# Idle TensorE products between the first dispatch products, and five tiles' rows kept until most of a table is written

## The chip, the cores and the metric

The kernel runs on one core of a Trainium2 chip. The time is the device time of one execution in microseconds; the median of three runs is the measure. Besides the timed runs there is one execution with a profile.

## The reference

```python
def reference(q, k, v, ...):
    attn = local_attention(q, k, v) + pooled_attention(q, k, v)      # 4 x 8 heads x 576 x 64
    x = attn.transpose(0, 2, 1, 3).reshape(2304, 512)
    x = soft_moe(x, phi, moe_w1, moe_w2)                             # 8 experts x 4 slots
    # second layer of experts: two of eight for each token
    noisy = x @ w_gate + log1p(exp(x @ w_noise)) * noise
    top2, top2_w = two largest of noisy and their softmax
    for e in range(8):
        for k in range(2):
            mask = top2[:, k] == e
            out[mask] += top2_w[mask, k, None] * (relu(x[mask] @ w1[e]) @ w2[e])
    return out                                                       # 2304 x 512
```

Both edits lie in the second layer of experts (w1 is 512 x 1024, w2 1024 x 512 for each expert).

## The kernel before, in words

Attention and the first layer of experts fill the first 212 us. Since every token is then a mixture of 32 slots, the second layer works on the mixing weights: `stk` holds for each of 18 token tiles of 128 tokens a row per token with those weights, the gates and the token's number, 128 numbers in all. For each expert up to 640 tokens (`CAP`) are collected, 128 x 5 tiles. So there are 40 output tiles, `tile2(e, ti)` for expert e and ti from 0 to 4. Each is a row of 24 products of 512 columns on TensorE into a PSUM tile `y` (two buffers), and between them the instructions of the list `fill[ti]` are issued, spread evenly: this is how all other work is ordered by hand. Instructions run in the order of issue on each engine.

How tokens are collected:

- Experts 0 and 1: by products. `onehot(e, n)` lets VectorE compare a token tile's ranks with a ramp, `dispatch(e, n)` multiplies `stk` with the result on TensorE. For expert 0 the one-hots 0 to 9 and their dispatches run ahead of the first output tile (L1178, L1185), the others, 10 to 17, lie in tile 0's list, which is written out as `FILL0` (`f` first layer, `w` split of w2, `o` one-hot, `s` scatter, `g` product for expert 1, `d` dispatch).
- Experts 2 to 7: through a table `tab` in DRAM. `places` works out a row number for each token and choice, then 36 `scatter`s (an indirect DMA of 128 rows issued by GpSimd, each behind a small memset called `spacer`) write `stk` into the table: eight by FILL0, 28 by the list `SCAT`, whose entries (tile, from, to) put scatters into the lists of tiles 1 to 6 (tile number 5e + ti). `xfetch(e)` reads 640 rows into a tile `XT` (two buffers), `turn` transposes them on TensorE, `gathered` copies them to `XS` on ScalarE, `first_layer` multiplies and applies relu. For expert 2, xfetch lies in tile 8's list, turn, gathered and first_layer in tile 9's. The read waits for all scatters, and on SyncE's queue reads of later experts' weights stand behind it.

At the end of `tile2` ScalarE writes the tile times its gates to `ys` (three buffers), and `add_out` adds its rows to the output: an indirect DMA with an add, issued by GpSimd. Output rows of one expert differ, so `add_out` lifts the dependence on the add just before it within the expert:

```python
        if ti:
            tc.declare_no_dep(st.ins, AD[e, ti - 1].ins, reason="an expert has a token once")
```

All other adds to the output keep their order by waiting. The list `OUTS` holds tiles whose add has not been issued yet: in the kernel before, tiles 0 and 1 of expert 0 are kept and added behind tile 2, and every later tile is added at once.

`spin(n)` issues n products of 512 bf16 columns into a `y` buffer that nobody reads. `SPIN[5]` of them stand behind the first dispatches.

Of the kernel before, what the change touches and what calls it, by code (L numbers as in the profile page):

```python
# [7 lines left out]
F32 = mybir.dt.float32  # L8
# [30 lines left out]
def attn_moe_moe_kernel(ctx: ExitStack, tc: tile.TileContext, q, k, v, moe_phi, moe_w1, moe_w2,  # L39
# [4 lines left out]
    DM = H * D  # L44
# [42 lines left out]
    for r in range(0, out.shape[0], 512):  # L87
        n = min(512, out.shape[0] - r)
# [27 lines left out]
    with ExitStack() as tctx:  # L116
# [48 lines left out]
        LD, VQ, KD, DQ, SD, SS, PD, PL, XL, XT, XK = ({} for _ in range(11))  # L165
# [470 lines left out]
        for nm in TSEQ:  # L636
# [4 lines left out]
            else:  # L641
                n, u = nm.split(":")
# [173 lines left out]
    wkp = sctx.enter_context(tc.tile_pool(name="ewk", bufs=2, reuse_waits="tile"))  # L816
# [81 lines left out]
    def dispatch(e, n):  # L898
        i = ORD[n]
        lo, hi = WIN[i]  # L900
        if n == 0:
            XP[e] = [ps.tile([128, n], F32, name=f"xs{c}", bufs=1) for c, (_, n) in enumerate(CH)]
        oh = OH.pop((e, n))
        c1 = CH[1][0]
        if lo < c1:
            nc.tensor.matmul(XP[e][0][:, lo:min(hi, c1)], stk[:, i], oh[:, 0:min(hi, c1) - lo], start=(n == 0),
                             stop=True, skip_group_check=True)
        if hi > c1:
            nc.tensor.matmul(XP[e][1][:, max(lo, c1) - c1:hi - c1], stk[:, i], oh[:, max(lo, c1) - lo:hi - lo],
                             start=(i == FIRST1), stop=True, skip_group_check=True)  # L910

    def gathered(e, part=(1, 0)):
        if e not in XS:
            XS[e] = wkp.tile([128, CAP], F32R, name="XS", bufs=1)
        for c in part:
            c0, n = CH[c]
            nc.scalar.activation(XS[e][:, c0:c0 + n], XP[e][c], AF.Copy)
# [23 lines left out]
    XFS = (3, 4)  # L941
    OHG = ()
    WSA = {0: (6, 8, 10, 12, 14, 16), 1: (2, 5, 8, 11, 14, 17)}
    SCAT = [(1, 8, 14), (2, 14, 19), (3, 19, 24), (4, 24, 28), (5, 28, 32), (6, 32, 36)]

    def places():

# [27 lines left out]
    XT = {}  # L975
# [33 lines left out]
    def tile2(e, ti, fill):  # L1009
        c = 0 if 128 * ti < CH[1][0] else 1  # L1010
        nf = len(fill)
        lead = LEAD0 if e == 0 and ti == 0 else 0
        for i in range(lead):
            fill[i]()
        done = lead
        hh, hl = HH[e, c]
        whi, wlo = WS[e]
        ts_ = slice(128 * ti - CH[c][0], 128 * ti - CH[c][0] + 128)
        y = ps.tile([128, DM], F32, name="y")
        for m in range(24):  # L1020
            kk, li = divmod(m, 3)
            l, r_ = ((hh, whi), (hh, wlo), (hl, whi))[li]
            nc.tensor.matmul(y, l[:, kk, ts_], r_[:, kk], start=(m == 0), stop=(m == 23))  # L1023
            while done < nf and (done - lead) * 24 < (m + 1) * nf:
                fill[done]()
                done += 1
        ys = wkp.tile([128, DM], F32, name="ys", bufs=3)
        gt, idx = ME[e]
        nc.scalar.activation(ys, y, AF.Copy, scale=gt[:, ti:ti + 1])  # L1029
        OUTS.append((e, ti, ys))  # L1030
        if e or ti >= 2:
            while OUTS:
                add_out(*OUTS.pop(0))

    OUTS = []

# [2 lines left out]
    def add_out(e, ti, ys):  # L1039
        gt, idx = ME[e]  # L1040
        nc.gpsimd.memset(spacer, 0.0)  # L1041
        st = nc.gpsimd.indirect_dma_start(out=out, out_offset=bass.IndirectOffsetOnAxis(ap=idx[:, ti:ti + 1], axis=0),  # L1042
                                          in_=ys, in_offset=None, compute_op=ALU.add)
        if ti:
            tc.declare_no_dep(st.ins, AD[e, ti - 1].ins, reason="an expert has a token once")
        AD[e, ti] = st
        if (e, ti) in DRAINS:
            nc.gpsimd.drain()  # L1048

    def spin(n):  # L1050

        t = ps.tile([128, DM], F32, name="y") if n else None
        for _ in range(n):
            nc.tensor.matmul(t, onesb, onesb[:, None].to_broadcast([128, 4, 128]), start=True, stop=True)
# [12 lines left out]
    NOH = LAST0 + 1  # L1067
    LEAD0 = 3

    with ExitStack() as gctx:  # L1070
# [13 lines left out]
        t = ps.tile([128, 2 * E], F32, name="h")  # L1084
# [7 lines left out]
        for q_ in range(5):  # L1092
            n = min(4, NTILE - 4 * q_)
# [64 lines left out]
        for i in range(NTILE - 1):  # L1158
            n = NTILE - 1 - i
# [24 lines left out]
            f()  # L1184
        for n in range(NOH):  # L1185
            dispatch(0, n)
        spin(SPIN[5])
        gathered(0, (0,))
        if PLP is None:
# [24 lines left out]
    for e in range(E):  # L1214
# [3 lines left out]
        def add(i, fn, *a):  # L1218
            fill[i].append(lambda: fn(*a))
# [57 lines left out]
        if e == 3:  # L1277
            add(1, spill)
            add(2, spill_n)
        for sl, n0, n1 in SCAT:  # L1280
            if sl // 5 == e:
# [3 lines left out]
        for ti in range(5):  # L1285
            tile2(e, ti, fill[ti])
# [5 lines left out]
    with tc.If(ov > 0):  # L1292
        with ExitStack() as octx:
# [6 lines left out]
            with tc.For_i(0, E, 1) as ei:  # L1300
# [13 lines left out]
                for i in range(NTILE):  # L1314
# [12 lines left out]
                    ys = ow.tile([128, DM], F32, name="oys")  # L1327
# [36 lines left out]
```

## Time and profile before

| | us |
|---|---|
| median of three runs | 514.25 |
| lowest, highest | 513.48, 517.23 |
| profiled execution | 509.43 |
| its span, first to last instruction | 506.9 |

The mean granted clock of TensorE over the span is 0.948 of full speed. Times in rows are microseconds from the start of the span; PE is TensorE, PEld its weight load, DVE VectorE, ACT ScalarE, POOL GpSimd, SP SyncE, a q behind a name means that engine's sequencer; L1042 is line 1042 of the kernel. A matmul's shown duration includes its way through the array, so that neighbouring ones overlap; the distance between two starts is what one costs. The releaser that a row names is inferred and can be wrong where several things were waited for.

### The profile page before, as it was taken

The numbers are of one execution on the slowest core, as the hardware profiler recorded it, in microseconds if no ns is written. First come the engines' busy times: TensorE is split into PE (matmuls) and PEld (weight loads), VectorE is DVE, ScalarE is ACT, GpSimd is POOL, SyncE is SP. The second block draws the span as 40 slices with busy tenths as digits, with TensorE's granted clock in tenths as the row PEclk, the third lists the DMA queues.
The fourth block names the chain that finished last, engine by engine and source line by source line (L and its number), as shares of the span: only waits on it lengthen the run. The fifth ranks groups of instructions, "written<-read, shape, count | busy, mean of one in ns | idle before, by whom it ended". The sixth has DMA issues, their size and how long they took to land.

```text
span 506.9 us, 12610 instructions
## 1 busy us (share of the span) xinstructions
PE 462.6 (91%) x4869; PEld 350.5 (69%) x4869; DVE 277.8 (55%) x682; ACT 284.5 (56%) x728; POOL 209.6 (41%) x321
## 2 busy tenths in 40 slices
PE   5787889899698899999999989999999999999993
PEld 4676657767566544446888768788787887878882
DVE  7786566888776432089677326265462552634400
ACT  3788566798687311265556356384662755636410
POOL 4666444656545100128878861322122222222222
PEclk9889877999988999887999999999999999999998
DMA  8999999999999799999994369896856867333333
GB/s 190 279 249 273 229 223 243 256 221 236 270 225 321 272 326 396 395 358 288 354 333 76 65 177 348 260 313 138 233 127 166 255 102 195 43 43 41 41 44 44
DMA packets 89672, 109.56 MB, mean 216 GB/s; under 512 B 30666, under 2 KB 59338, under 8 KB 89610
## 3 DMA queue, kind: packets, MB, share of 16 engines
q1 hardware_dynamic: 82698, 95.87, 64.3%
q0 software_dynamic: 6912, 12.85, 16.8%
q8 instruction: 40, 0.66, 0.6%
q14 instruction: 22, 0.18, 0.1%
HBM read 88.64 MB, written 20.05 MB: 214 GB/s over the span
## 4 chain that ended last, share of the span: by engine, by line
PE 58%; DMA 18%; issue 6%; POOL 6%; DVE 5%; ACT 4%; POOLq 1%; SPq 1%; ACTq 0%; DVEq 0%
PE y L1023 34%; DMA ld<-in_q_dram 5%; DMA wr<-in_moe_w_dram 4%; DMA vq<-in_v_dram 4%; PE yacc L776 3%; DMA ld<-in_k_dram 3%; POOL tab L969 3%; PE hp L754 3%; POOL out_dram L1042 2%; PE gx L828 2%; PE t L214 2%; PE h L1003 2%; PE gx L1003 2%; DMA V<-in_v_dram 1%; POOLq L1048 1%
## 5 line engine op out<-in xcount | busy, mean ns | idle before, releaser
L1023 PE MATMUL y<-whi,hl 128*128 128x512 f32 x320 | 127.7, 399 | 0.0
L1023 PE MATMUL y<-wlo,hh 128*128 128x512 f32 x320 | 127.6, 399 | 0.0
L1023 PE MATMUL y<-whi,hh 128*128 128x512 f32 x320 | 126.8, 396 | 0.3 <-ACT hh L1004 0.3
L1042 POOL DMA_INDIRECT out_dram<-ys,idx x40 | 64.4, 1611 | 114.5 <-ACT ys L1029 63.9
L995 DVE TENSOR_TENSOR wlo<-wr,whi 128x512 fp32r<-128x512 f32 x64 | 41.9, 691 | 54.1 <-ACT whi L992 53.8
L1023 PEld LDWEIGHTS y<-wlo,hh 128*128 128x128 f32 x320 | 60.5, 189 | 13.9 <-issue 1.2
L1029 ACT ACTIVATE ys<-y,gt 128x512 f32<-128x512 f32 x40 | 27.4, 685 | 74.6 <-issue 40.2
L1023 PEld LDWEIGHTS y<-whi,hl 128*128 128x128 f32 x320 | 60.5, 189 | 11.9 <-issue 1.6
L1023 PEld LDWEIGHTS y<-whi,hh 128*128 128x128 f32 x320 | 60.5, 189 | 11.7 <-ACT hh L1004 0.6
L1005 DVE SCALAR_TENSOR_TENSOR hl<-h,hh 128x256 fp32r<-128x256 f32 (+1 forms) x64 | 31.4, 490 | 21.4 <-ACT hh L1004 19.8
L969 POOL DMA_INDIRECT tab<-stk,pos x36 | 36.5, 1015 | 8.4 <-issue 7.6
L294 POOL TENSOR_TENSOR P<-El,su 64x350 f32<-64x350 f32 x31 | 24.1, 778 | 37.8 <-DVE su L287 28.8
L1004 ACT ACTIVATE hh<-h 128x256 fp32r<-128x256 f32 (+1 forms) x64 | 27.9, 436 | 16.4 <-PE h L1003 14.4
L992 ACT ACTIVATE whi<-wr 128x512 fp32r<-128x512 f32 x64 | 36.9, 625 | 0.2
L1005 DVE SCALAR_TENSOR_TENSOR hl<-gx,hh 128x256 fp32r<-128x256 f32 (+1 forms) x64 | 31.3, 489 | 10.2 <-ACT hh L1004 8.1
L1004 ACT ACTIVATE hh<-gx 128x256 fp32r<-128x256 f32 (+1 forms) x64 | 28.0, 438 | 15.2 <-PE gx L1003 12.9
L214 PE MATMUL t<-idf,ld 96*128 96x96 f32 x192 | 23.5, 269 | 12.6 <-DMA ld<-in_k_dram 8.1
L1041 POOL MEMSET spacer<- 1x1 f32 x40 | 18.2, 454 | 39.5 <-issue 39.5
L202 ACT ACTIVATE K<-t 64x288 f32<-64x288 f32 x64 | 27.4, 428 | 8.0 <-PE t L214 6.5
L202 ACT ACTIVATE PT<-t 64x256 f32<-64x256 f32 (+1 forms) x50 | 20.6, 416 | 17.8 <-PE t L336 16.9
L214 PEld LDWEIGHTS t<-idf,ld 96*128 96x128 f32 x192 | 19.0, 153 | 16.6 <-DVE mask L141 3.7
L226 DVE TENSOR_REDUCE Dq<-Q 64x144 f32<-64x576 f32 x32 | 23.9, 747 | 10.2 <-ACT Q L202 9.5
(293 smaller groups left out, 828.8 us busy)
## 6 DMA issues: line engine op xcount, KB each, us to landing
wr<-in_moe_w_dram SPq DMA_DIRECT2D x120, 256.0 KB
wr<-in_moe_w_dram SPq DMA_DIRECT2D x56, 512.0 KB
out_dram<-zero SPq DMA_DIRECT2D x5, 1024.0 KB
V<-in_v_dram SPq DMA_DIRECT2D x62, 80.0 KB
ld<-in_k_dram SPq DMA_DIRECT2D x16, 288.0 KB
ld<-in_q_dram SPq DMA_DIRECT2D x16, 288.0 KB
vq<-in_v_dram SPq DMA_DIRECT2D x16, 288.0 KB
tab<-zero SPq DMA_DIRECT2D x1, 1920.0 KB
```

Source lines behind the costliest of these rows:

```text
L202: nc.scalar.activation(dst, src, AF.Copy)
L214: nc.tensor.transpose(t[:, c:288:3], ld[:, i, h, 128 * c:128 * c + 128], idf[0:96, 0:96])
L226: nc.vector.tensor_reduce(out=Dq[hs, :, h], in_=Q[hs, h, 0:576].rearrange("p (a n r) -> p a n r", a=3, r=4), axis=AX.X, op=ALU.add)
L294: eng.tensor_tensor(P[as_, :, HQ * a:HQ * a + KW], El[as_], su[as_, :, None].to_broadcast([64, NG, KW]), op=ALU.mult)
L969: st = nc.gpsimd.indirect_dma_start(out=tab, out_offset=bass.IndirectOffsetOnAxis(ap=pos[:, c, i:i + 1], axis=0), in_=stk[:, i].bitcast(F3 ...
L992: nc.scalar.activation(whi[:, kk], wb(kk), AF.Copy)
L995: eng.tensor_tensor(wlo[:, kk], wb(kk), whi[:, kk].bitcast(F32), op=ALU.subtract)
L1004: nc.scalar.activation(hh[:, f], h, AF.Relu)
L1005: nc.vector.scalar_tensor_tensor(hl[:, f], h, 0.0, hh[:, f].bitcast(F32), op0=ALU.max, op1=ALU.subtract)
L1023: nc.tensor.matmul(y, l[:, kk, ts_], r_[:, kk], start=(m == 0), stop=(m == 23))
L1029: nc.scalar.activation(ys, y, AF.Copy, scale=gt[:, ti:ti + 1])
L1042: st = nc.gpsimd.indirect_dma_start(out=out, out_offset=bass.IndirectOffsetOnAxis(ap=idx[:, ti:ti + 1], axis=0), in_=ys, in_offset=None, c ...
```

## The change

Behind each of the first nine dispatches of expert 0 one idle product is issued, two behind the first. The first five tiles are kept: tiles 0 and 1 in buffers of XT, which stand empty until tile 8, the others in ys. At tile 4 the adds of tiles 0 to 2 are issued, at tile 5 that of tile 3, at tile 6 those of tiles 4 to 6, and from tile 7 on each at once. (`SCAT[-1][0]` is 6.) The list of the scatters starts with five instead of six in tile 1, so that tile 4 has five instead of four.

```diff
--- before.py
+++ after.py
@@ -941,7 +941,7 @@
     XFS = (3, 4)
     OHG = ()
     WSA = {0: (6, 8, 10, 12, 14, 16), 1: (2, 5, 8, 11, 14, 17)}
-    SCAT = [(1, 8, 14), (2, 14, 19), (3, 19, 24), (4, 24, 28), (5, 28, 32), (6, 32, 36)]
+    SCAT = [(1, 8, 13), (2, 13, 18), (3, 18, 23), (4, 23, 28), (5, 28, 32), (6, 32, 36)]
 
     def places():
 
@@ -1024,13 +1024,16 @@
             while done < nf and (done - lead) * 24 < (m + 1) * nf:
                 fill[done]()
                 done += 1
-        ys = wkp.tile([128, DM], F32, name="ys", bufs=3)
+        if e == 0 and ti < 2:
+            ys = wkp.tile([128, 5, 128], F32, name="XT").rearrange("p t d -> p (t d)")[:, 0:DM]
+        else:
+            ys = wkp.tile([128, DM], F32, name="ys", bufs=3)
         gt, idx = ME[e]
         nc.scalar.activation(ys, y, AF.Copy, scale=gt[:, ti:ti + 1])
         OUTS.append((e, ti, ys))
-        if e or ti >= 2:
-            while OUTS:
-                add_out(*OUTS.pop(0))
+
+        while len(OUTS) > (5 if 5 * e + ti < 4 else 2 if 5 * e + ti < SCAT[-1][0] else 0):
+            add_out(*OUTS.pop(0))
 
     OUTS = []
 
@@ -1184,6 +1187,8 @@
             f()
         for n in range(NOH):
             dispatch(0, n)
+            if n + 1 < NOH:
+                spin(1 + (n == 0))
         spin(SPIN[5])
         gathered(0, (0,))
         if PLP is None:
```

## Rows read from the trace of the kernel before

**Rows 1.** The page: busy time, share of the span and instructions of each engine.
```profile
PE 462.6 (91%) x4869; PEld 350.5 (69%) x4869; DVE 277.8 (55%) x682; ACT 284.5 (56%) x728; POOL 209.6 (41%) x321
```

**Rows 2.** Waits of TensorE, 230 us to the end: us, times, longest.
```profile
PE xs L984 <- DMA XT<-tab: 1.6, 1, 1.6
```

**Rows 3.** The chain that ended last, 290 to 300 us: start, us, what.
```profile
294.59 2.25 DMA tab<-stk,pos
296.86 3.17 DMA XT<-tab
```

**Rows 4.** GpSimd's timeline, 259 to 300 us: start us, us, instruction, idle before it.
```profile
259.82 2.10 POOL L1042 DMA_INDIRECT out_dram<-ys,idx  x1 [0.22 <-ACT whi L992]
...
266.15 1.57 POOL L1042 DMA_INDIRECT out_dram<-ys,idx  x1 [2.25 <-ACT whi L992]
...
268.02 0.99 POOL L969 DMA_INDIRECT tab<-stk,pos  x1 [0.26 <-issue]
...
293.32 0.96 POOL L969 DMA_INDIRECT tab<-stk,pos  x1 [0.22 <-issue]
...
294.59 0.95 POOL L969 DMA_INDIRECT tab<-stk,pos  x1 [0.23 <-issue]
...
295.85 1.62 POOL L1042 DMA_INDIRECT out_dram<-ys,idx  x1 [0.23 <-issue]
...
297.77 2.11 POOL L1042 DMA_INDIRECT out_dram<-ys,idx  x1 [0.27 <-ACT whi L992]
```

**Rows 5.** Windows, 229 to 236 us: busy by engine; granted clock, DMA share, GB/s.
```profile
229.40:236.20 6.80, 6.49 (x19) 5.07 (x20) 6.58 (x13) 3.19 (x8) 5.53 (x12) 0.50 1.05 296
```

**Rows 6.** TensorE's timeline, 221 us: idle products.
```profile
220.84 1.47 PE L1054 MATMUL y<-onesb 128*128 128x512 bf16 x6
```

**Rows 7.** TensorE's timeline, 228 us: dispatch products.
```profile
228.11 0.36 PE L906 MATMUL xs<-oh,stk 128*128 128x192 f32 x1 [0.24 <-DVE oh L891]
...
228.75 0.36 PE L906 MATMUL xs<-oh,stk 128*128 128x192 f32 x1 [0.23 <-DVE oh L891]
```

**Rows 8.** Windows, 225 to 242 us: the third busy time is VectorE.
```profile
225.05:233.00 7.95, 6.35 (x30) 4.08 (x20) 7.95 (x15) 5.25 (x14) 6.96 (x13) 0.78 1.03 302
233.00:242.40 9.40, 9.40 (x50) 6.86 (x50) 8.97 (x22) 4.37 (x11) 7.66 (x14) 0.83 1.02 282
```

**Rows 9.** Adds (L1042): all; those issued at 259.82, 302.09, 316.95; a wait.
```profile
DMA to landing us min/median/max: 4.7/4.9/9.0
...
DMA to landing us min/median/max: 5.6/5.6/5.6
...
DMA to landing us min/median/max: 9.0/9.0/9.0
...
DMA to landing us min/median/max: 7.3/7.3/7.3
...
L1042 POOLq EVENT_SEMAPHORE  x1: 3835/3835/3835, 297.5 to 297.5; - x1
```

**Rows 10.** Windows, 265 to 305 us: busy by engine; granted clock, DMA share, GB/s.
```profile
265.00:296.00 31.00, 31.00 (x167) 24.65 (x166) 15.82 (x33) 17.06 (x38) 25.03 (x43) 1.00 0.42 76
297.00:305.00 8.00, 6.37 (x33) 4.90 (x32) 2.54 (x8) 3.75 (x10) 4.26 (x6) 1.00 0.90 248
```

**Rows 11.** ScalarE's timeline: ys of tile 8 and the copies of XS behind it.
```profile
298.12 0.67 ACT L1029 ACTIVATE ys<-y,gt 128x512 f32<-128x512 f32 x1
302.29 0.77 ACT L917 ACTIVATE XS<-xs 128x384 fp32r<-128x384 f32 x2 [3.50 <-PE xs L984]
```

**Rows 12.** SyncE's timeline: the reads behind that of XT.
```profile
297.34 8.28 SPq L108 DMA_DIRECT2D wr<-in_moe_w_dram  x12
```

**Rows 13.** TensorE's timeline: start of tile 9; expert 2's first-layer product.
```profile
297.83 0.39 PE L1023 MATMUL y<-whi,hh 128*128 128x512 f32 x1
...
303.27 0.28 PE L1003 MATMUL h<-XS,GS 128*128 128x256 f32 x1
```

**Rows 14.** Windows, 140.6 to 144.1 us: granted clock before the DMA share.
```profile
140.60:144.10 3.50, 3.50 (x59) 2.77 (x61) 1.96 (x3) 3.21 (x11) 1.22 (x3) 0.51 1.15 225
```

## Prediction

> **What bounds the kernel now.** I read the page first: TensorE is busy for 91% of the span, VectorE, ScalarE and GpSimd for 41 to 56% [rows 1]. Then I asked what TensorE waits for from 230 us to the end, because both edits lie there. One wait counts: 1.6 us of the first transpose of XT (L984) for the read of the table [rows 2]. So from 232 us to the end the time is TensorE's own work, and an edit moves the end by what it moves TensorE. The chain of waits says what stood behind that one wait: the last scatter is issued at 294.59 and lands 2.25 us later, and the read of the table takes 3.17 us [rows 3]. GpSimd's timeline shows scatters and adds without a pause for 28 us before it, at 1.27 us for a scatter and 1.9 us for an add [rows 4]. Last I read the granted clock around the first dispatch: it is at the lower level (1.2 GHz) from 229.4 to 236.2 [rows 5].
>
> All times below are in the profiled execution: 506.9 us of span, 509.43 us with what lies around it, 0.9% under the median of the three timed runs (514.25). I work out a difference and put it on the median.
>
> I number the tiles t = 5e + ti. add(t) is `add_out` of tile t, ys(t) the scaled tile that it reads.
>
> **The idle products (first edit).** Ten more products of 512 columns. At full clock one costs 0.245 us (six in 1.47 [rows 6]), at the lower level twice that, 0.49. The dispatch products of tiles n = 4 to 7 follow each other every 0.63 us, and TensorE sits idle for 0.22 to 0.26 us before each, waiting for VectorE's one-hot; two of the four are shown [rows 7]. One idle product fits that gap at full clock and costs nothing; at the lower level it is 0.25 us too long, nine times that is 2.2 us at most. What the edit can bring is the clock: 6.8 us at half rate hold 3.4 us of full-rate work. But VectorE doesn't speed up with TensorE. It is busy for 7.95 of 7.95 us from 225.05 to 233.00, and for 8.97 of 9.40 us from there to 242.4, by which its last one-hot of expert 0 is done [rows 8]; FILL0 ends with the dispatches that need those one-hots. So of the 3.4 us only VectorE's idle time, 0.4 us, can come back in this stage. I take a gain of 0.4 us, with bounds of 2.2 us lost (clock not held) and 3.4 us gained (VectorE not the limit after all).
>
> **The adds (second edit), step by step on GpSimd's queue.** The scatters wait for no other engine, so they run at their own pitch. Before, add(0) starts at 259.82 behind 19 scatters, and add(2) only at 266.15 [rows 4]. Why so late? add(t) is excused from waiting for add(t-1) alone, so it waits for add(t-2) to land: add(0) took 5.6 us [rows 9], to 265.4, and add(2) follows 0.74 us later. The same pattern shows further on: a wait on GpSimd's queue begins at 297.5 and lasts 3.84 us, to 301.35 [rows 9]; so add(6), issued at 295.85 [rows 4], was 5.5 us on its way and add(8) waited for it.
> After the change scatter 19 takes the place at 259.82, and scatter 27 starts 8 x 1.27 later, at 269.98. add(0) follows at 271.24 (1.26 behind a scatter), add(1) 1.92 later at 273.16. add(0) lands in some 4.8 (the median of all adds is 4.9 [rows 9]; the DMA engines are at 0.42 then [rows 10]), so add(2) starts at 276.76, scatters 28 to 31 from 278.63 (1.87 behind an add) to 282.44, add(3) at 283.70, scatters 32 to 35 from 285.57 to 289.38. That is 5.2 us ahead of 294.59: two adds fewer in front, and the pause before add(2), which is still there, takes the place of the old one. The last scatter lands at 291.6, XT at 294.8. TensorE wants it at 298.4. **The wait of 1.6 us is gone**, by over 3 us.
>
> **What is late next.** Adds 4, 5 and 6 now stand in a heap behind the last scatter. add(4) starts at 290.64. add(5) is the first of expert 1 and may meet rows of expert 0, so it waits for add(4) to land. ys has three buffers, and with tiles 0 and 1 kept elsewhere ys(t) still waits for add(t-3) to land, from tile 5 on. Before, none of these waits showed on TensorE. After:
> add(4) starts 1.0 us ahead of the read of XT, just as add(6) did before, which needed 5.5: 296.1. add(5) starts 0.74 later, 296.9. On SyncE the read of XT has twelve weight reads queued behind it, which start 0.5 us after it [rows 12], so now near 292 instead of 297.34; add(5) flies in their midst. The price of such a flight is not shown as such. Lower bound 4.8 (DMA engines at 0.42), upper bound 9.0 (add(8), which was queued behind another add); adds that started alone among weight reads took 5.6 (at 259.82) and 7.3 (at 316.95) [rows 9]. I take 6.4, between those two: add(5) lands at 303.3 (301.7 to 305.9).
> ys(5), ys(6) and ys(7) are held on ScalarE until 281.5, 288.5 and 296.1 by adds 2, 3 and 4, but TensorE needs their PSUM bank only two tiles on, ys(7)'s for tile 9 at 297.83 [rows 13]: no cost, with 1 us to spare. ys(8) is another matter. On ScalarE's queue the two copies of XS (L917, `gathered`) stand directly behind it [rows 11], and TensorE's first product of expert 2's first layer needs XS. ys(8) at 303.4, XS from 304.0 to 304.8, the product at 305.0 (0.2 behind XS, as before [rows 11, 13]). Before, this product ran at 303.27; without the wait for XT and with the 0.4 us above it could run at 301.2. So TensorE stands for 3.8 us, and **the product is 1.7 us later than before**, between 0.1 and 4.3 by the bounds for add(5).
> After 3.8 us of idleness the clock may fall. The nearest rows: 1.63 us of waiting at 298.4 left it at full rate [rows 10]; of the stretches at the lower level one lasted 3.5 us [rows 14], one 6.8 [rows 5]. At half rate they cost 1.7 and 3.4 us, but some of it can lie within the idle time itself. I take 1.0, bounds 0 and 3.4.
> Beyond tile 9 nothing is added: ys(9) waits for add(6), which starts 1.9 us behind add(5), and isn't wanted before tile 9's 24 products are done.
>
> The sum: +1.7 +1.0 = **+2.7 us**, 512.1 in a profiled execution, **517.0** on the median. The gain of the first edit is not in it: TensorE arrives 0.4 us sooner at a wait that GpSimd sets.
>
> A page prices the flight of an add otherwise. The Trainium skill, "DMA: Bandwidth & Descriptors", section "Anatomy of one DMA — SWDGE (gpsimd) path", fits a DMA issued by GpSimd as 2.0 us plus its bytes over 436 GB/s. For 128 rows of 2 KB that is an estimate of 2.6 us; two such flights would put ys(8) at 296.6, no wait would be left, and the result would be the first rival's. The rows say 4.7 at the least [rows 9], so I don't use it.
>
> **Rivals.** (1) *The change does what it says*: add(5) has landed when ys(8) wants its buffer (299.4 with TensorE sooner). That takes two flights in 299.4 - 290.64 - 0.74 = 8.0 us, 4.0 each, and no add in the trace took under 4.7; my timetable for GpSimd would have to be 1.5 us late as well. Then 1.6 + 0.4 are won: 512.2. If VectorE is no limit either, 5.0 are won, 509.2; more than that is not in the two waits. (2) *A draw*: add(5) flies 4.8 to 5.2, the product runs at 303.4 to 303.8, TensorE stands for 2.4 us and the clock holds: +0.3, 514.5. (3) *Slower*: the heap of adds costs the wait it saves several times over. add(5) needs 9.0, as add(8) did at the same distance from the read of XT; the product runs at 307.6, +4.3; 6.4 us of idleness bring the lower clock for 6.8 us, +3.4: 521.9. It decides once add(5) takes more than 7.5 us and the clock falls. Against it: that add(8) was queued behind add(7), while add(5) starts alone.
>
> **Chances.** My forecast 0.50; (1) 0.12; (2) 0.20; (3) 0.18. A measurement of this kernel, whose three runs differ by 0.7%, can tell about 1% (5.1 us) from nothing. Only the far end of (1) is faster than that: 0.04. (3) is slower: 0.18. The rest, 0.78, is within 1%. The range goes from the near end of (1) to most of (3): 511.8 to 521.0.
>
> **What would show it.** In the changed kernel's trace: the last scatter near 289.4 and XT read near 291.6; no wait of L984 for the table; a wait of TensorE of some 4 us at L1003 in tile 9, with ScalarE's ys(8) released by an add's landing near 303; granted clock at full rate from 229 to 236, but VectorE through with its one-hots at most 0.5 us sooner than 242.4. I am wrong if ys(8) is not held, if add(5) doesn't wait for add(4), or if tile 1 starts 2 us sooner, which would say that VectorE was not the limit.

## The result and the profile after

| | before | after |
|---|---|---|
| median of 20 runs each, us | 513.4 | 519.42 |
| lowest, highest | 508.55, 525.16 | 515.45, 524.58 |
| profiled execution (span) | 509.43 (506.9) | 519.2 (517.0) |
| ratio after to before | | 1.0126, 95% interval 1.0099 to 1.0152 |

The change costs 6.5 us (513.4 x 0.0126; 5.1 to 7.8 by the interval). The ratio leaves out runs of more than 1.5% above the fastest of their kernel (three of the twenty of after), so that it isn't the ratio of the two medians, 1.0117. The forecast was +2.7. The sign is right and the time lies in the range, but near its upper end, which is 6.75 us over 514.25, and on the third rival's side of the 1% line, to which I gave 0.18.

The page of after first: span, and busy time by engine. Against [rows 1] TensorE has ten products more and hardly more busy time (463.3 against 462.6 us), in a span 10.1 us longer.

```profile
span 517.0 us, 12632 instructions
...
PE 463.3 (90%) x4879; PEld 350.9 (68%) x4879; DVE 276.7 (54%) x682; ACT 284.5 (55%) x728; POOL 210.6 (41%) x321
```

Not all of these 10.1 us belong to the change. The first one-hot of expert 0 runs at 225.05 us in the profiled execution of before and at 226.06 in that of after, and nothing of the change lies ahead of it. From here on I count times from that instruction, written with a plus sign, wherever two kernels are compared. From there to the end of the span before takes 281.9 us and after 290.9: 9.0 us in these two executions, 6.5 by all runs.

The waits of TensorE in after, 230 us to the end (engine, tile and line, what was waited for; us in all, times, longest), to be held against the one of [rows 2]:

```profile
PE h L1003 <- ACT XS L917: 4.5, 1, 4.5
PE y L1023 <- ACT ys L1032: 2.4, 1, 2.4
PE y L1023 <- ACT hh L1004: 0.4, 1, 0.4
```

The wait for the table (L984, 1.6 us) is gone. Two others stand in its place, both for ScalarE. TensorE's timeline shows where (start, us, instruction, idle time before it in brackets): tile 9's first product and expert 2's first first-layer product.

```profile
300.63 0.50 PE L1023 MATMUL y<-whi,hh 128*128 128x512 f32 x1 [2.36 <-ACT ys L1032]
...
310.50 0.58 PE L1003 MATMUL h<-XS,GS 128*128 128x256 f32 x1 [4.45 <-ACT XS L917]
```

ScalarE's timeline says that it was itself held, from ys(5) on each time by the landing of an add. The rows are ys(6), ys(7), ys(8) and the copies to XS behind it ([rows 11] in before):

```profile
291.40 0.69 ACT L1032 ACTIVATE ys<-y,gt 128x512 f32<-128x512 f32 x1 [5.76 <-DMA out_dram<-ys,idx]
...
299.89 0.69 ACT L1032 ACTIVATE ys<-y,gt 128x512 f32<-128x512 f32 x1 [6.76 <-DMA out_dram<-ys,idx]
...
309.11 0.69 ACT L1032 ACTIVATE ys<-y,gt 128x512 f32<-128x512 f32 x1 [3.66 <-DMA out_dram<-ys,idx]
309.69 0.76 ACT L917 ACTIVATE XS<-xs 128x384 fp32r<-128x384 f32 x2
```

And GpSimd's timeline holds the cause: two of the slower scatters, then add(2), the last scatter (292.05), add(4), add(5) and add(6). Before, the last scatter stood at 294.59 [rows 4].

```profile
259.55 1.23 POOL L969 DMA_INDIRECT tab<-stk,pos  x1 [0.23 <-issue]
...
261.08 1.20 POOL L969 DMA_INDIRECT tab<-stk,pos  x1 [0.23 <-issue]
...
278.93 1.56 POOL L1045 DMA_INDIRECT out_dram<-ys,idx  x1 [2.01 <-ACT hh L1004]
...
292.05 0.95 POOL L969 DMA_INDIRECT tab<-stk,pos  x1 [0.22 <-issue]
...
293.31 2.11 POOL L1045 DMA_INDIRECT out_dram<-ys,idx  x1 [0.21 <-ACT whi L992]
...
300.63 1.59 POOL L1045 DMA_INDIRECT out_dram<-ys,idx  x1 [5.17 <-ACT ys L1032]
...
302.53 1.58 POOL L1045 DMA_INDIRECT out_dram<-ys,idx  x1 [0.26 <-issue]
```

GpSimd sits idle for 5.17 us before add(5), though scatters are over and tile 5 is long done. The releaser in the brackets is an instruction that happened to end near; what it waits for is add(4), which the groups of these two adds show, each alone in a window (us from issue to landing, add(4) then add(5)):

```profile
DMA to landing us min/median/max: 6.5/6.5/6.5
...
DMA to landing us min/median/max: 8.4/8.4/8.4
```

293.31 + 6.48 = 299.79, and ys(7) starts 0.1 us later, add(5) 0.84 later. 300.63 + 8.39 = 309.02, and ys(8) starts 0.09 us later. These two flights in a row, 14.9 us, set when TensorE goes on. (A flight is the time from the issue of an add to its landing.)

Last the windows around both edits (us; busy time by engine with counts; granted clock of TensorE, DMA share, GB/s). In the first two, the lower level of [rows 5] is gone; the stretches from 301.0 and from 308.9 at less than full clock are new:

```profile
226.00:234.00 8.00, 7.19 (x43) 4.04 (x35) 7.97 (x16) 5.55 (x14) 6.96 (x13) 1.00 1.04 304
230.30:237.20 6.90, 5.97 (x28) 4.07 (x27) 6.90 (x15) 4.10 (x11) 5.63 (x12) 1.00 1.05 299
...
301.00:305.40 4.40, 4.40 (x17) 3.29 (x16) 2.00 (x5) 4.29 (x10) 2.88 (x4) 0.62 1.05 405
305.60:308.80 3.20, 0.45 (x2) 0.01 (x1) 0.98 (x5) 0.00 (x0) 0.00 (x0) 1.00 1.07 307
308.90:315.70 6.80, 5.20 (x15) 4.42 (x16) 2.23 (x6) 3.64 (x9) 3.21 (x4) 0.50 1.07 349
```

TensorE runs at half rate behind both waits. The first such stretch costs nothing, since TensorE stands waiting behind it anyway. Of the second, 5.2 us (310.50 to 315.71) hold work that everything later waits for: at half rate that is 2.6 us lost.

### The profile page after: what moved, and what is told of

It is laid out like the page before. It is cut to its first block, busy times and chain, and to the rows that moved or that the text cites. A ratio compares the mean times of both kernels' runs of the same rounds, so it can differ in the third digit from the quotient of the medians.

```text
span 517.0 us, 12632 instructions
## 1 busy us (share of the span) xinstructions
PE 463.3 (90%) x4879; PEld 350.9 (68%) x4879; DVE 276.7 (54%) x682; ACT 284.5 (55%) x728; POOL 210.6 (41%) x321
## 5 line engine op out<-in xcount | busy, mean ns | idle before, releaser
L1045 POOL DMA_INDIRECT out_dram<-ys,idx x38 | 60.8, 1599 | 121.9 <-ACT ys L1032 66.0
L1032 ACT ACTIVATE ys<-y,gt 128x512 f32<-128x512 f32 x38 | 26.1, 686 | 83.1 <-issue 36.9
L969 POOL DMA_INDIRECT tab<-stk,pos x36 | 37.9, 1052 | 8.3 <-issue 7.8
L214 PE MATMUL t<-idf,ld 96*128 96x96 f32 x192 | 24.6, 276 | 12.0 <-DMA ld<-in_k_dram 7.1
L253 PE MATMUL S<-K,Q 128*32 128x35 f32 x1280 | 17.7, 206 | 17.8 <-issue 13.3
L214 PEld LDWEIGHTS t<-idf,ld 96*128 96x128 f32 x192 | 20.0, 159 | 16.6 <-DVE mask L143 4.3
```

Source lines behind the costliest of these rows:

```text
L214: nc.tensor.transpose(t[:, c:288:3], ld[:, i, h, 128 * c:128 * c + 128], idf[0:96, 0:96])
L969: st = nc.gpsimd.indirect_dma_start(out=tab, out_offset=bass.IndirectOffsetOnAxis(ap=pos[:, c, i:i + 1], axis=0), in_=stk[:, i].bitcast(F3 ...
```

## Experiments

The table counts from the first one-hot: the last scatter, the first first-layer product of expert 2 (L1003, the place where the two kernels part), and the end of the span. "after" in an edit means that the change is in, with the one thing altered.

| kernel | last scatter | L1003 product | end | time against before | ratio, 95% interval |
|---|---|---|---|---|---|
| before | +69.5 | +78.2 | +281.9 | | |
| after | +66.0 | +84.4 | +290.9 | 519.42, 513.4 | 1.0126 [1.0099, 1.0152] |
| e1 idle products only | +70.7 | +79.4 | +282.7 | 515.36, 515.67 | 1.0003 [0.9961, 1.0044] |
| e2 adds only | +65.3 | +82.7 | +288.2 | 520.65, 515.67 | 1.011 [1.0017, 1.0203] |
| e3 after, two more buffers | +66.5 | +75.7 | +279.0 | 509.53, 515.67 | 0.9892 [0.9806, 0.9977] |
| e4 before, tile 5 kept | +69.2 | +77.7 | +281.7 | 512.23, 515.67 | 0.9929 [0.9885, 0.9972] |
| e9 after, weight reads later | +66.0 | +80.3 | +294.5 | 525.44, 514.15 | 1.0268 [1.0182, 1.0354] |
| e10 after, add(4) a tile sooner | +68.3 | +77.2 | +280.2 | 512.55, 514.15 | 0.9953 [0.9911, 0.9995] |

### The two edits apart: e1 and e2

e1 is before with the idle products alone; e2 is after without them.

```diff
 # e1, on before
             dispatch(0, n)
+            if n + 1 < NOH:
+                spin(1 + (n == 0))
 # e2, on after
             dispatch(0, n)
-            if n + 1 < NOH:
-                spin(1 + (n == 0))
```

> The first edit alone (idle products between the dispatches; adds as before). My theory: VectorE limits the stretch, so tile 1 starts 0.7 us sooner, as in the changed kernel, the clock stays at full rate there, and TensorE then waits 0.7 us longer for the table (2.3 us instead of 1.6), because GpSimd sets that: no change in time (-0.5 to +0.3 us). Rival: the idle products delay the dispatches and are part of what was lost: 1.5 us or more slower, tile 1 later than before. Second rival: the clock's 3.4 us come through: 2 us or more faster.

> The second edit alone (kept tiles; no idle products). My theory: all of the loss is here, since GpSimd's chain of scatters, add(4), add(5) sets the product of expert 2's first layer: 5 to 7.5 us slower than the kernel before, with waits of TensorE at tile 9's start and at L1003 that together are 0.7 us shorter than in the changed kernel, and the lower clock from 229 to 236 back. Rival: the idle products share in the loss: under 4 us slower.

e1 measures the same as before (by its interval 2.0 us faster to 2.3 slower); e2 is slower by 1.1%, 0.9 to 10.5 us by a wide interval, 6.3 us in its trace. So the loss is the second edit's in the main; a small share of the first is not excluded. In e1 the windows of the stretch show full clock and VectorE without a gap (7.95 of 7.95 us, then 8.64 of 8.70, up to the end of the last one-hot):

```profile
228.15:236.10 7.95, 7.41 (x48) 4.51 (x47) 7.95 (x15) 5.50 (x14) 6.96 (x13) 1.00 1.10 326
236.10:244.80 8.70, 8.32 (x49) 5.59 (x48) 8.64 (x22) 3.92 (x10) 6.94 (x14) 1.00 1.03 287
```

The last one-hot of expert 0 ends 0.67 us sooner than before (+16.59 for +17.26), ys(0) 0.73 sooner: the clock came back and brought little, since VectorE was already busy. Then TensorE waits longer for the table, 3.5 us where I expected 2.3, as add(0) flew 6.5 us in this execution and pushed the last scatter to +70.7. TensorE's wait in e1, and the window around it, at full clock:

```profile
PE xs L984 <- DMA XT<-tab: 3.5, 1, 3.5
...
300.00:312.00 12.00, 8.49 (x44) 6.73 (x43) 4.84 (x13) 5.51 (x14) 4.89 (x6) 1.00 0.86 249
```

In e2 the old stretch at half rate is back (+5.2 to +12.0), and the wait at tile 9 isn't there. The wait at L1003 is 5.7 us, 1.1 less than the two waits of after together, and a new stretch at half rate begins in it; 4.4 us of this stretch hold work:

```profile
PE h L1003 <- ACT XS L917: 5.7, 1, 5.7
...
310.30:317.10 6.80, 4.37 (x13) 3.69 (x14) 1.70 (x4) 3.21 (x8) 3.21 (x4) 0.50 1.07 352
```

### The chain of two flights: e3 and e10

If ys(7) and ys(8) are held because their buffers are in flight, two more buffers take both waits away, whatever the adds do. e3 puts them where nobody needs the data any more:

```diff
 # e3, on after
+        elif 5 * e + ti == 7:
+            ys = LK.rearrange("p t s -> p (t s)")[:, 0:DM]
+        elif 5 * e + ti == 8:
+            ys = iot[:, 0:DM]
         else:
             ys = wkp.tile([128, DM], F32, name="ys", bufs=3)
```

> Both edits, but tiles 7 and 8 are scaled into two buffers that stand empty by then, so that no ys waits for add(4) or add(5); GpSimd's queue, the heap of adds and the weight reads stay. My theory: both waits of TensorE vanish, the clock stays, the wait for the table is gone too: 1.6 + 0.7 = 2.3 us faster than the kernel before (1.5 to 3), some 9 us under the changed kernel. Rival: the heap of adds costs through the DMA engines, the weights or XT come late whatever the buffers: still 3 us or more slower than before.

It beats both kernels: 0.9892 of before. No wait at L984, L1003 or tile 9 is left. ScalarE's timeline shows the two tiles written with no idle time before them:

```profile
294.99 0.68 ACT L1036 ACTIVATE LK<-y,gt 128x512 f32<-128x512 f32 x1
...
300.47 0.67 ACT L1036 ACTIVATE iot<-y,gt 128x512 f32<-128x512 f32 x1
```

Yet add(5) still waits for add(4) (it starts 6.5 us behind it, in after 7.3), and the two adds fly 5.7 and 9.1 us (groups, each add alone; add(4) is issued at 295.57):

```profile
DMA to landing us min/median/max: 5.7/5.7/5.7
...
DMA to landing us min/median/max: 9.1/9.1/9.1
```

The flights alone cost nothing, then; what cost was that a buffer hung on them. The trace gives a gain of 2.9 us on before, counted from the first one-hot (2.5 of them at L1003), the runs one of 5.6 (515.67 x 0.0108) with a wide interval, 1.2 to 10.0; 2.9 lies in it.

e10 keeps the buffers and takes one flight out of the chain: add(4) is issued at tile 5, ahead of the last four scatters, so that its flight passes under them.

```diff
 # e10 (and e6), on after
-        while len(OUTS) > (5 if 5 * e + ti < 4 else 2 if 5 * e + ti < SCAT[-1][0] else 0):
+        while len(OUTS) > (5 if 5 * e + ti < 4 else 2 if 5 * e + ti < 5 else 1 if 5 * e + ti < 6 else 0):
```

> The changed kernel, but the add of tile 4 goes out with that of tile 3 at tile 5, in front of the last four scatters; tiles 5 and 6 are still added behind them. My theory: add(5) finds add(4) landed and starts right behind the last scatter, so one flight of 6 to 9 us is taken out of the chain, at the price of a scatter chain 1.9 us longer: ys(7) isn't held, the product at L1003 is 0 to 2 us later than in the kernel before, and the time within -1 to +3 us of it. Rival: it isn't the chain of two flights but the flight of add(5) alone: 5 us slower, as the changed kernel.

> The kernel of e6 once more, for the same reason. My theory: add(4) has landed when the last scatter is out, add(5) follows it within 1.3 us, ys(7) isn't held, tile 9 starts without a wait, and the wait at L1003 falls from 4.5 us to 0 to 2.5, by add(5)'s flight alone; time -1 to +3 us against the kernel before. Rival: the flight of add(5) alone holds ys(8) as long: wait of 4 us or more, 5 us slower.

GpSimd's timeline of e10: add(5) now follows the last scatter without a pause, and lands after 5.72 us, at 308.86.

```profile
301.88 0.96 POOL L969 DMA_INDIRECT tab<-stk,pos  x1 [0.22 <-issue]
...
303.14 1.62 POOL L1045 DMA_INDIRECT out_dram<-ys,idx  x1 [0.22 <-issue]
```

The first one-hot stands at 233.59 here, 7.5 us later than in after; counted from it, add(5) starts at +69.6 instead of +74.6. ys(8) still waits for it, but TensorE no longer waits for XS: no wait at L1003 is left, 1.3 us at L984 (the last scatter stands behind one add more than in after). The product runs at +77.2, 1.0 sooner than before, and the runs agree, just clear of the noise: 0.9953, where after was 1.0126. The edit alters two things: add(5) starts 5.0 us sooner, and its flight is shorter, 5.7 for 8.4, since it now starts ahead of the weight reads. With after's 8.4 and its 1.5 us from landing to product, the product would have come near +79.4 (an estimate), 1.2 later than before; so most of the 7.2 us between after and e10 is the first flight that no longer counts. The same kernel as e6 measured 1.0093 [1.0, 1.0185]; the gain is shown only where the disturbance of the last section is absent.

### Why the flight was long: e9

e9 moves the weight reads that stand behind the read of XT on SyncE's queue [rows 12] to a later tile and to another queue:

```diff
 # e9 (and e7), on after
-    WF = {1: (None, 1), 2: (4, 5), 3: (10, 9)}
+    WF = {1: (None, 1), 2: (4, 5), 3: (None, None)}
...
+        if e == 2:
+            add(0, lambda: wfetch(3, (1, 0), eng=nc.scalar))
```

> The changed kernel, but the twelve reads of expert 3's weights, which stood behind the read of XT on SyncE, are issued by ScalarE in tile 10. My theory: the adds fly long because of those reads: add(4) lands in 4.8 instead of 6.5, add(5) in 4.8 to 5.5 instead of 8.4, the product at L1003 comes 4.5 to 5.5 us sooner and the clock falls for a shorter time or not: within -0.5 to +2 us of the kernel before. Rival: adds in a heap fly long by themselves: still 5 us or more slower.

> The kernel of e7 once more, read in its trace from the last scatter to the first product of expert 2's first layer, since e7's execution lost 14 us in tile 1 already and nothing was held afterwards. My theory: with no weight reads behind XT, add(4) and add(5) land in 4.8 to 5.5 us each (6.5 and 8.4 in the changed kernel), tile 9 starts without a wait, and the wait at L1003 is 0 to 1.5 us. What the late reads cost later, from tile 11 on, isn't part of the question. Rival: adds in a heap fly long by themselves: add(5) needs 8 us or more.

As a kernel it is worse, since the late reads make TensorE wait for weights afterwards (5.5 us at L828 and more). The reading is the stretch around the adds. GpSimd's timeline: add(4), add(5).

```profile
293.86 2.00 POOL L1045 DMA_INDIRECT out_dram<-ys,idx  x1 [0.22 <-issue]
...
300.65 1.59 POOL L1045 DMA_INDIRECT out_dram<-ys,idx  x1 [4.75 <-ACT ys L1032]
```

ScalarE's timeline: two copies of weights end at 305.46 and ys(8) starts there, with no idle time before it.

```profile
304.33 1.15 ACT L992 ACTIVATE whi<-wr 128x512 fp32r<-128x512 f32 x2
305.46 0.69 ACT L1032 ACTIVATE ys<-y,gt 128x512 f32<-128x512 f32 x1
```

So add(5), issued 0.5 us sooner than in after as counted from the first one-hot, had landed by 305.46: 4.8 us at the most, for 8.4 among the reads. (The next read of XT, issued at 302.55 in after, has also gone from beside it: here it runs at once behind the first, at 294.95.) When the weight reads did run, later, the adds beside them took 9.7 and 10.8 us. add(4) took 5.9 us against 6.5: it flies beside the read of XT in both, so the weight reads explain little of its flight. The product came at +80.3 instead of +84.4, still 2.0 later than before: the expectation missed there, with 1.8 us of waiting at tile 9 and 2.6 at L1003. What is left is add(4): ys(7) is held by it until 299.91, and from there to XS ScalarE works without a pause.

### The other side of the trade: e4

If the adds in front of the last scatter cost, keeping one more tile in *before* must already help, with no tile held for long.

```diff
 # e4, on before
-        if e or ti >= 2:
+        if (e or ti >= 2) and 5 * e + ti != 5:
```

> The kernel before, with one add moved: that of tile 5 is issued behind tile 6's scatters. My theory: one add fewer in front of the last scatter, which is issued 1.9 us sooner; the wait for the table falls from 1.6 us to 0; add(5) doesn't wait for add(4), which has long landed, so ys(8) is held for 1 to 4 us at most and TensorE's product at L1003 not or by under 1 us: 0.8 to 1.6 us faster. Rival: any add behind the scatters flies among the weight reads and holds ys(8): slower by 1 to 4 us, with a wait at L1003.

0.9929, a gain of 3.7 us by the runs (1.4 to 5.9). The trace shows less: the wait at L984 is 0.9 us for 1.6, the product 0.5 us sooner. In this execution add(0) took 7.5 us for 5.6, and add(2) came 1.7 us later than before (+42.8 for +41.1), so that the last scatter was only 0.3 us sooner instead of the expected 1.9. The rival didn't come: ys(8) is held for 2.9 us (+76.0 for +73.1), but no wait at L1003 follows.

### VectorE as the limit of the first edit: k1 and k2

Both are before without the lower halves of half of the weights of expert 0's second layer; k2 has the idle products too.

```diff
-            l, r_ = ((hh, whi), (hh, wlo), (hl, whi))[li]
+            l, r_ = ((hh, whi), (hh, wlo if e or kk < 4 else whi), (hl, whi))[li]
...
-            step = {"f": lambda n: first_layer(0, 0, n), "w": lambda n: wsplit(0, n, "v"), "o": lambda n: onehot(0, n),
+            step = {"f": lambda n: first_layer(0, 0, n), "w": lambda n: wsplit(0, n, "v", (0,)), "o": lambda n: onehot(0, n),
```

> The kernel before with less work for VectorE in tile 0: for expert 0 the lower halves of w2's blocks 4 to 7 aren't made (four subtractions of 0.69 us), and their products use the upper halves instead, so these outputs are less exact; TensorE's work is the same. My theory: TensorE runs at the lower clock from 229 to 236 and is the limit together with VectorE; tile 1 starts 0.3 to 1 us sooner than before, counted from the first one-hot. Rival (VectorE is the only limit): 2.5 us sooner.

> The same with the idle products between the dispatches (the same lower halves are left out). My theory: with VectorE relieved the full clock pays: tile 1 starts 2 to 3.4 us sooner than in the kernel before, against 0.7 with VectorE's full work. Rival: something else than VectorE, such as ScalarE's relus, is the limit: 1 us or less.

k1 gave no reading (see the last section). In k2 the stretch is whole up to the last one-hot: it ends at +15.9, against +16.6 in e1 and +17.3 in before, and VectorE has 1.4 us of idle time up to there. That is 1.4 us of gain, not the 2 to 3.4 that I expected once VectorE was relieved, and ys(0) is no sooner than in e1 (+18.64 for +18.68). So VectorE is a limit, and something else comes close behind it; I take it for TensorE's own order of work, which these runs don't show by itself. There is one execution of each.

### Without a reading: e5 to e8

e5 is e1 and e4 together; e6 and e7 are the kernels that e10 and e9 ran again; e8 puts 18 idle products of 384 columns into the wait at L1003, to tell the clock's share from the wait's.

```diff
 # e8, on after
+    def fill_in():
+        t = ps.tile([128, 384], F32, name="h")
+        for _ in range(18):
+            nc.tensor.matmul(t, onesb, onesb[:, None].to_broadcast([128, 3, 128]), start=True, stop=True)
...
+            if nx == ET:
+                add(s1, fill_in)
```

> The kernel before with the idle products and with the add of tile 5 moved behind tile 6's scatters. My theory: the 0.7 us of the first edit come through once TensorE no longer waits for the table: 1.5 to 2.3 us faster than before. Rival: they don't add up, because the table comes just in time for one of them: 0.8 to 1.6 us, as with the moved add alone; or ys(8) is held and there is a loss.

> The changed kernel with 18 idle products of 384 columns in front of expert 2's first layer, where TensorE stands for 4.5 us. They take 2.9 us at full clock, 5.8 at half. My theory: they lie within the wait, and the lower clock behind it (6.8 us from 308.9) doesn't come: 2 to 3 us faster than the changed kernel, +3 to +4.5 us against the kernel before. Rival: the clock has no share in the loss, which is the wait alone: no difference from the changed kernel, or a loss where the products outlast the wait.

They ran beside runs of before that themselves took 527.4 us, where it had 513 to 516 beside the kernels of the table (and 527.9 beside k1 and k2). Measured: e5 527.45, 0.9993 [0.9948, 1.0038]; e6 538.34, 1.0093 [1.0, 1.0185]; e7 541.8, 1.0263 [1.0205, 1.0321]; e8 542.02, 1.0245 [1.018, 1.031]. In their traces TensorE stands for 7 to 15 us at the longest in tile 0 or 1, far ahead of the wait in question, while GpSimd goes on; so GpSimd is ahead of its timetable afterwards, and no ys waits for an add. e8's wait at L1003 wasn't there to be filled. The share of the clock thus has no experiment of its own; it rests on rows.

## Why the prediction was right in sign and short in size

**What bounds it.** As read: TensorE's order of work, with single waits that move the end. In after the product at L1003 is 6.2 us later than before (+84.4 for +78.2) and the end 9.0.

**The idle products.** Right in the mechanism, small in size. Forecast 0.4 us, and 0.5 at most at the last one-hot, because VectorE is full; measured 0.68 there, 0.73 to 0.75 at ys(0), in e1 and in after alike. Half of it is VectorE's idle time, 0.33 us before and none now; the other half is that its same 35 instructions fill 16.6 us instead of 16.9, which no run explains. It is in neither result, since TensorE arrives that much sooner at a wait that GpSimd sets. e1 measures no difference, as said.

**The last scatter.** Right in direction, too large in size: 5.2 us sooner was forecast, 3.5 came. I let scatters run at their pitch of 1.27 us throughout; in after seven of the eight from 256.39 to 266.95 are longer themselves, 1.05 to 1.43 us instead of 0.96, and follow each other at up to 1.7 us (259.55 to 261.08 is 1.53). The DMA share was 1.05 around one pair of them and 0.13 around another, so the load of the DMA engines is not the whole reason; no run looks for it. It is not one execution's accident: add(0), forecast for +46.2, starts between +47.0 and +47.4 in after, e2, e3, e9 and e10. With this add(4) came 1.7 us behind my timetable. The wait for the table is gone all the same.

**What is late next.** The mechanism is the one forecast, instruction by instruction: add(2) 0.74 us behind add(0)'s landing (in after as in before), add(5) behind add(4)'s, ys(8) behind add(5)'s, XS behind ys(8), TensorE at L1003. e3 and e10 show that it is the cause: with either edit to the chain the loss is gone and a gain stands in its place, 1.1% and 0.5%.

**The terms that failed** are, first, the price of the two flights, and then the late start of add(4). The product was forecast 1.7 us later than before and came 6.2 later, outside the bounds of 0.1 to 4.3, which let add(5)'s flight alone vary; the 4.5 between are add(4)'s late start, 1.7, its flight, 1.0 (6.5 for 5.5), the distance to add(5), 0.1, and add(5)'s flight, 2.0 (8.4 for 6.4), less 0.2 behind ys(8). I took 6.4 as a middle between adds that flew alone among weight reads. The upper bound, 9.0, was the nearer row, since add(8) flew at the same distance from the read of XT; I set it aside because add(8) was queued behind another add. I overlooked that the adds on either side of it were long as well: add(7), issued at 297.77, and add(9), issued at 307.98, in before (groups, each add alone):

```profile
DMA to landing us min/median/max: 8.3/8.3/8.3
...
DMA to landing us min/median/max: 8.1/8.1/8.1
```

Being alone wasn't the point: in after and in e9 alike add(6) is issued 1.9 us behind add(5), and e9 shows that the reads are enough, 8.4 with them, at most 4.8 without.
A price of 2.6 us, the estimate from the Trainium skill, "DMA: Bandwidth & Descriptors", section "Anatomy of one DMA — SWDGE (gpsimd) path", is far from every flight measured here, the shortest of which took 4.4 us (e1); the measurement decides.

**"No cost, with 1 us to spare" for ys(7)** failed too, by the same term: add(4) landed at 299.79, and tile 9 waited 2.36 us. On the end of after this costs nothing of its own, since the wait for XS ends later anyway; in e9, where add(5) lands early, it is what keeps the product 2.0 us late.

**The clock.** Forecast 1.0 us, bounds 0 and 3.4; read from the rows 2.6. Together the product's 6.2 and the clock's 2.6 make 8.8 of the 9.0 us that the profiled executions differ by. The other traces bear this out: from the L1003 product to the end, e1, e3, e4 and e10, without half rate behind the product, differ from before by -0.7 to +0.2 us, after by +2.8, and e2, whose 4.4 us at half rate are worth 2.2, by +1.7. The length of the stall alone doesn't foretell it: 2.36 us in after and 2.58 in e9 were followed by 3.4 us at half rate, e1's 3.51 at L984 by none. The runs say 6.5, and at most 7.8 (513.4 x 0.0152): these two executions lie further apart than the kernels do, and no run shows by which term.

**The rival.** Rival (3) named both conditions, add(5) over 7.5 us and the lower clock, and both held. I gave it 0.18. It priced itself at +7.7; the runs say +6.5. Of the two accounts it was the better one, and that the time still fell into the forecast's range is owed to the width of the range.

## What to carry to other kernels

Before moving work behind a deadline, list what was spread out and will now stand in a heap, and ask which buffers hang on it: here two more buffers of 128 x 512 made a version 1.1% faster than before (0.2 to 1.9%) out of one 1.3% slower. Where two dependent transfers follow each other, take for each flight the row measured beside the same neighbours, here the weight reads, rather than a middle, since both errors add up. A stall of TensorE can cost more than its length: stalls of 2.36, 2.58, 4.45 and 5.74 us here brought 3.4 to 6.8 us at half rate, one of 3.51 us none. Give such a stretch a term of its own, with bounds.

## What was not expected of the hardware

An add of the same 128 rows of 2 KB took between 4.4 us (e1) and 10.8 us (e9, when the late reads ran), and its length goes with what the DMA engines move beside it. Of the 254 adds whose landing the traces of all these kernels show, the 203 with less than 215 GB/s in their flight took 4.4 to 6.5 us, but for one of 8.1; of the 47 with more than 250 GB/s, 44 took over 7. The issue of a scatter on GpSimd, 0.96 us as a rule, can take up to 1.6 (1.05 to 1.43 in the rows above, at a DMA share of 1.05 and of 0.13).

In e5 to e8, k1 and k2 TensorE, VectorE and ScalarE each stood for several microseconds in tile 0 or 1, with no releaser that the profile names or one that had long been done. Two rows of e5, of ScalarE's and TensorE's timelines:

```profile
260.94 0.49 ACT L1004 ACTIVATE hh<-h 128x384 fp32r<-128x384 f32 x1 [5.17 <-remote]
```

```profile
262.74 0.48 PE L906 MATMUL xs<-oh,stk 128*128 128x128 f32 x1 [9.86 <-DVE oh L891]
```

The windows of e5: in 25 us TensorE is busy for 13.4, GpSimd for 17.8, and the DMA engines are full.

```profile
240.00:265.00 25.00, 13.44 (x48) 9.60 (x49) 6.85 (x18) 6.61 (x13) 17.83 (x32) 0.76 1.00 345
```

The kernels of e6 and e7 lost nothing there when they ran again as e10 and e9 (512.55 for 538.34, 525.44 for 541.8), and the unchanged kernel took 12 to 14 us longer beside e5 to e8 and k1 and k2 as well, so it isn't the edits alone. But e5 to e8 ran on one chip, k1 and k2 on a second, e1 to e4 on a third, e9 and e10 on a fourth; whether the cause lies in the chip, in the moment or elsewhere stays open.
